# A mixer kernel whose list scheduler also picks the buffers, with the sign step split between GpSimd and VectorE and token weights placed first

## The chip, the core and the metric

The kernel runs on one core of one Trainium2 chip. The metric is the device time of one execution in microseconds (us). The core has five engines with a queue each, taken in order: TensorE (PE, with its weight loads as PEld), VectorE (DVE), ScalarE (ACT), GpSimd (POOL) and SyncE (SP), which here issues nearly all transfers. An instruction waits at the head of its queue until what it needs is there, and all that stand behind it on that engine wait too.

## What is computed

```python
def sm_attn(qq, kk, vv):                      # softmax(qq kk^T / 8) vv
    ...
q_d = q.reshape(B, H, Sd, factor, D).mean(axis=3)        # likewise k_d, v_d
out_up = np.repeat(sm_attn(q_d, k_d, v_d), factor, axis=2)
mask = np.abs(pos[:, None] - pos[None, :]) < factor
...
attn = np.exp(scores)
attn = attn / (np.sum(attn, axis=-1, keepdims=True) + 1e-09)
x = (out_up + np.matmul(attn, v))             # (B, S, H*D)
h = np.maximum(xt @ w_tok1, 0.0) @ w_tok2     # token mixing, xt = x^T
u = x + h.transpose(0, 2, 1)
h2 = np.maximum(u @ w_ch1, 0.0) @ w_ch2       # channel mixing
return (u + h2).astype(np.float32)
```

There are B = 8 batches of H = 8 heads, S = 576 tokens, D = 64, factor = 4 (so Sd = 144 pooled tokens). The token matrices are 576 x 256 and 256 x 576, the channel matrices c1 512 x 1536 and c2 1536 x 512. [...]

## The kernel before, in words

**Precision.** A product in the mixer is done in three passes (`mm3`, L103 to L105): each operand is held as a high and a low part, and high x high, high x low and low x high are summed. Channel mixing takes 16-bit parts (`f16`), token mixing `f32r` parts.

**A batch.** `qk` holds queries and keys, `vw` the values in windows, `vr` the values to be pooled. `pool_q` pools on DVE (L366, L368), `load_v` on POOL (L344, L345). Pooled attention runs over 4 pairs of heads (`pooled`: scores `sd`, maximum `mxd` L386, exponent `pd`, transposes `td` L398, copy `ptd` L401, product `ad` L407, division L413 to L415), and its result goes by a transfer issued on ACT's queue (L421) into `vw`, as one more row of the window. Local attention runs over 5 tiles of tokens (`local`: scores `sc` L439, mask and softmax on DVE L446 to L458, transposes `pT` L462, product `av` L475, copy to `x` L480). Then `mix`: split x into `xh` (L512, L514), product with w_tok1 into `t`, relu and split into `hid` (L529, L531), then for two chunks of 256 and 320 tokens the product with w_tok2 on top of a transpose of x (L545), the copy `u` (L552) and the maximum of |u| (`umx`, L554). `everywhere` brings that maximum to all partitions by two small PE steps (`um_t` L491, `um_b` L497) and two on DVE (L488, L494); `pow2` (L107 to L111) makes a power of two `us` of it, and `uh` is u in two f16 parts (L567 on ACT, L569 on DVE). Channel mixing is `first` (12 blocks f of 12 matmuls into `c`, then `h` on ACT L644 and DVE L646) and `second` (4 blocks c of 36 matmuls from `h` into `c`, then the addition to u, L672, and the store).

**Weights.** A raw tile of 128 x 512 doubles is 512 KB. `to_f32` (L169) takes the high words on ACT (L175), the low words on POOL (L178), and joins them on DVE by a shift (L180); `signed` (L182) adds the sign on DVE (L184). So each tile takes two passes of DVE. Token weights (`token_weight`, 5 pieces of w_tok1 and 4 of w_tok2) are then split into `W` (L213, L215). Channel weights (`Channel.stage`, 12 tiles of C1 and 12 of C2) land in `CW`; PE sums their magnitudes with a matrix of ones (L279, L288), DVE takes the maximum of the sums (L283, L291), and one scale `C_s` for all of C1 (L262 to L264), and one for C2, is used to make the two f16 parts of each tile (`CW`, ACT L268 and DVE L270). W and C1 share the five raw buffers `h`, two loads in flight for each; C2's raw tiles lie in the `vw` buffers.

**What sets the order.** Each part is a generator that yields a `step(engine, us, needs, take, give)` ahead of the instructions it emits. `drive` (L136) keeps model clocks for the engines and picks, again and again, the step that can start first by them, within `PATIENCE` = 0.3 us by the order of the list `streams`. So it writes one fixed order for every engine, from the start until channel products of batch 0 are done (`("over", 0, 1)`): batch 0, all weights, and as much of batch 1 as fits. Its clocks decide the order alone; on the chip every engine takes its queue in that order. PSUM tiles come from three tags, `gg` (2), `m` (3) and `g` (1), which rotate. After `drive`, a plain loop over batches 1 to 7 writes `first` and `second` and puts pieces of the next batch's attention and mixing between the products (`tick`, with `SIDE` = 42).

## Time and profile before

| | us |
|---|---|
| three runs: median (lowest, highest) | 976.34 (975.58, 978.17) |
| the profiled execution's own time | 977.24 |
| its span in the trace | 975.5 |
| time beside the span (977.24 - 975.5) | 1.74 |
| PE busy in the span | 907.9 |
| DVE, ACT, POOL busy in the span | 506.0, 301.1, 112.4 |

The profiled execution took 0.90 us more than the median. In the rows of the profile a group is named by its line, engine, operation, the tile written and the tiles read; "xN" is the number of instructions; a releaser behind "<-" is what ended the idle time before it. A row of windows gives, for a stretch of time, each engine's busy time, then the TensorE clock that was granted, the share of the DMA engines in use and GB/s. The page's second part cuts the span into 40 slices of 24.4 us; a digit is tenths of that slice.

### The profile page before, as it was taken

Reading aid. Unit: us, or ns where it says so; the run is one execution under the profiler, and the core shown is the slowest. Engines: PE = TensorE matmul, PEld = TensorE weight load, DVE = VectorE, ACT = ScalarE, POOL = GpSimd, SP = SyncE. Lnnn points to the kernel's source line nnn. Section 1 sums busy time; section 2 is a strip of 40 time slices with the busy share of each in tenths; the row PEclk is TensorE's granted clock in tenths of the full one; section 3 lists DMA queues with packets and bytes.
Section 4 is the critical chain, followed back from the end, with each engine's and each line's share of the span. In section 5 each row is a group of like instructions: output and inputs, shape, how many; then the busy total and the mean of one; then the engine's idle time right before and its main releaser. Section 6 shows DMA issues by size and latency. Waiting matters only on the chain. (4 is left out here: it accounts for less than half of the span.)

```text
span 975.5 us, 25542 instructions
## 1 busy us (share of the span) xinstructions
PE 907.9 (93%) x11292; PEld 712.2 (73%) x11292; DVE 506.0 (52%) x1187; ACT 301.1 (31%) x627; POOL 112.4 (12%) x213
## 2 busy tenths in 40 slices
PE   5747789999999999999999999999999999999998
PEld 4634467778867778677877778777876778777876
DVE  7879899244645354724555354724645345533221
ACT  1544456212323232422333232422432222322110
POOL 7143500030030003000120003000120000000000
PEclk9976799999999999999999999999999999999999
DMA  8266610530025002500133002600034000000000
GB/s 225 96 234 239 217 31 2 159 90 21 26 61 158 22 8 76 168 7 21 38 107 100 15 14 72 171 1 28 20 84 140 15 15 20 18 2 21 18 12 28
DMA packets 28221, 68.28 MB, mean 70 GB/s; under 512 B 3504, under 2 KB 14000, under 8 KB 26864
## 3 DMA queue, kind: packets, MB, share of 16 engines
q1 hardware_dynamic: 25552, 64.30, 21.9%
q10 hardware_dynamic: 2560, 2.36, 0.9%
q8 instruction: 88, 1.44, 0.6%
q14 instruction: 21, 0.17, 0.1%
HBM read 54.85 MB, written 9.44 MB: 66 GB/s over the span
## 5 line engine op out<-in xcount | busy, mean ns | idle before, releaser
L105 PEld LDWEIGHTS <-CW 128*128 128x128 f16 x4608 | 435.7, 98 | 136.5 <-issue 15.3
L105 PE MATMUL c<-uh,CW 128*128 128x256 f16 (+1 forms) x2304 | 310.7, 288 | 7.0 <-DVE CW L270 4.4
L105 PE MATMUL c<-h,CW 128*128 128x256 f16 (+1 forms) x2304 | 304.5, 287 | 0.8 <-issue 0.7
L646 DVE SCALAR_TENSOR_TENSOR h<-c,h 128x256 f16<-128x256 f32 (+1 forms) x192 | 87.3, 455 | 133.0 <-ACT h L644 131.9
L644 ACT ACTIVATE h<-c 128x256 f16<-128x256 f32 (+1 forms) x192 | 78.4, 408 | 211.2 <-PE c L105 211.0
L344 POOL TENSOR_TENSOR vr<-vr 72x256 f32<-72x256 f32 x64 | 49.0, 765 | 489.4 <-DMA vr<-in_vr_dram 298.1
L672 DVE SCALAR_TENSOR_TENSOR u<-c,io,u 128x256 f32<-128x256 f32 (+1 forms) x64 | 33.0, 516 | 109.7 <-PE c L105 109.7
L554 DVE TENSOR_REDUCE umx<-t 128x1 f32<-128x256 f32 (+1 forms) x64 | 29.2, 457 | 84.5 <-ACT u L552 84.4
L105 PE MATMUL t<-W,hid 128*128 128x256 f32 (+1 forms) x384 | 71.6, 323 | 0.0
L105 PE MATMUL t<-xh,W 128*128 128x512 f32 (+1 forms) x240 | 68.2, 419 | 1.1 <-ACT x L480 0.8
L552 ACT COPY u<-t 128x256 f32<-128x256 f32 (+1 forms) x64 | 25.5, 398 | 119.9 <-PE t L105 119.6
L105 PEld LDWEIGHTS t<-W,hid 128*128 128x128 f32 x384 | 56.7, 200 | 2.6 <-DVE hid L531 0.3
L105 PEld LDWEIGHTS t<-xh,W 128*128 128x128 f32 (+1 forms) x240 | 43.6, 192 | 12.5 <-issue 2.5
L475 PE MATMUL av<-vw,pt 47*32 47x64 f32 x2304 | 37.1, 233 | 14.6 <-ACT pt L466 4.4
L480 ACT COPY x<-av 128x512 f32<-128x512 f32 (+1 forms) x40 | 23.3, 582 | 88.4 <-PE av L475 80.9
L475 PEld LDWEIGHTS av<-vw,pt 47*32 47x32 f32 x2304 | 28.9, 110 | 25.2 <-issue 11.4
L567 ACT ACTIVATE uh<-u,us 128x256 f16<-128x256 f32 (+1 forms) x64 | 29.6, 524 | 49.0 <-DVE us L111 45.0
L407 PE MATMUL ad<-vd,ptd 72*72 72x65 f32 x512 | 42.5, 240 | 0.1
L407 PEld LDWEIGHTS ad<-vd,ptd 72*72 72x72 f32 x512 | 40.5, 157 | 1.3 <-ACT ptd L401 0.4
L545 PEld LDWEIGHTS t<-ident,x 128*128 128x128 f32 (+1 forms) x160 | 22.4, 146 | 18.4 <-issue 9.1
L545 PE MATMUL t<-ident,x 128*128 128x128 f32 (+1 forms) x160 | 33.0, 287 | 2.3 <-DVE umx L554 2.3
L569 DVE SCALAR_TENSOR_TENSOR uh<-u,us,uh 128x256 f16<-128x256 f32 (+1 forms) x64 | 31.1, 537 | 7.6 <-ACT uh L567 7.6
(84 smaller groups left out, 802.6 us busy)
## 6 DMA issues: line engine op xcount, KB each, us to landing
qk<-in_qk_dram SPq DMA_DIRECT2D x32, 579.0 KB
vw<-in_vw_dram SPq DMA_DIRECT2D x32, 351.0 KB
vr<-in_vr_dram SPq DMA_DIRECT2D x64, 144.0 KB
C_raw<-in_c_dram SPq DMA_DIRECT2D x12, 512.0 KB
C_raws<-in_c_dram SPq DMA_DIRECT2D x12, 512.0 KB
out_dram<-u SPq DMA_DIRECT2D x32, 160.0 KB
out_dram<-u SPq DMA_DIRECT2D x32, 128.0 KB
vw<-od ACTq DMA_DIRECT2D x32, 72.0 KB
```

The lines of the kernel that those rows point to most:

```text
L105: nc.tensor.matmul(ps, lhs(a), rhs(c), start=first and i == 0, stop=last and i == 2, **kw)
L344: nc.gpsimd.tensor_add(t[:, 0:2], t[:, 0:2], t[:, 2:4])
L407: nc.tensor.matmul(ps[:, g, par], pt[:, par, kg, G * g:G * g + G], st.vd[:, kg, 2 * pr + par], start=kg == 0, stop=kg == 1)
L475: nc.tensor.matmul(ps[QB * j:QB * j + QB, par, D * hp:D * hp + D], pt[p, hp, QB * j:QB * j + QB], st.vw[h][p, g, D * hp:D * hp + D], start ...
L545: nc.tensor.matmul(ps[:, o:o + n], xf(t)[:, 128 * c:128 * c + 128], ident[:n, :n], start=i == 0, stop=False, is_transpose=True, skip_group ...
L552: nc.scalar.copy(u, ps)
L554: nc.vector.tensor_reduce(umx[:, c:c + 1], ps, axis=AX.X, op=ALU.max, apply_absolute_value=True)
L567: nc.scalar.activation(t[:, 0], us[c], AF.Copy, scale=s)
L569: nc.vector.scalar_tensor_tensor(t[:, 1], us[c], s, t[:, 0], ALU.mult, ALU.subtract)
L644: nc.scalar.activation(ht[:, 0], ps, AF.Relu)
L646: nc.vector.scalar_tensor_tensor(ht[:, 1], ps, 0.0, ht[:, 0], ALU.max, ALU.subtract)
L672: nc.vector.scalar_tensor_tensor(us[c], banks[c], io, us[c], ALU.mult, ALU.add)
```

## The change

The part that `drive` orders is rebuilt; the loop over batches 1 to 7 keeps its form.

- **Buffers.** `drive` picks a numbered buffer for each PSUM tile and for `w` by its own clocks (`slot`, `free`, `held`). The raw tiles of C1 get a pool of their own, `cw` = 6; the token weights keep the five of `h`; of C2's raw tiles four lie in `qk` buffers and eight in `vw`. Loads are streams of their own (`weight_loads`, `Second.loads`), which wait only for a free buffer.
- **Signs.** `to_f32` does the sign by one instruction more, on POOL for every second tile (L214, which writes the sign bits of the 64-bit word's top 16 bits) and on DVE for the others (L217); then one DVE instruction (L219) joins and writes the result where it belongs.
- **Scales.** The sums of channel tiles are sums of squares (L304, L323). C1 has a scale for each quarter of four tiles (`First.scale`), and its f16 parts (L291, L293) are made a quarter at a time; C2 has one scale, after C1's. C2's f16 parts have a place of their own (`CX`, `CY`, in the `cw` buffers and one more).
- **Setup.** `masks` take 10 selects and 2 copies on POOL in place of 26 selects, and `rep` is a DVE sum (L105) in place of 8 selects.
- **Junk products.** `keep_busy` (L146 to L151) puts products of a tile of ones into PSUM tile `busy` that nobody reads, 14 at the start and up to 8 before a PE step for which the model clock shows a gap, until the last `uh` of batch 0.
- **Mixing.** `mix` is four generators (`splits`, `products`, `takes`, `scaled`). In `products` all of a batch's products with w_tok2 come in a row, and the maximum's way through PE (`um_t` L554, `um_b` L560) is in another.
- **Order.** The streams stand as loads, token weights, the tail of channel mixing, mixing, then C1, attention and the rest; `PATIENCE` is 0.15; the model's costs differ; `drive` ends when also batch 1's first `uh` is made.

```diff
-PATIENCE = 0.3
+SG = 2
+PATIENCE = 0.15
...
+    def keep_busy(n):
+
+        if n:
+            ps = P1("busy")
+            for _ in range(n):
+                nc.tensor.matmul(ps, junk[:, :128], junk, start=True, stop=True)
...
-            if e == "P" and ("uh", 0, 0) not in made:
-                us *= 1.8
+            if e == "P" and ("uh", 0, 1) not in made and free["g"]:
+                keep_busy(min(8, int((t - clock["P"]) * 0.6 / 0.22)))
...
-    def to_f32(raw, at):
+    def by_pool():
+        count[0] += 1
+        return count[0] * SG % 4 < SG
+
+    def to_f32(raw, at, y=None, *needs):
...
         nc.gpsimd.tensor_scalar(lo, lo, 2.0 ** -29, -0.501, ALU.mult, ALU.add)
-        yield step("V", 0.08 + n * 0.0012)
-        nc.vector.scalar_tensor_tensor(lo, hi, 3, lo, ALU.logical_shift_left, ALU.bitwise_or)
...
-        nc.vector.scalar_tensor_tensor(y, words[:, :, 1], 0x80000000, words[:, :, 0],
-                                       ALU.bitwise_and, ALU.bitwise_or)
+        if by_pool():
+            yield step("G", 0.08 + n * 0.0026)
+            nc.gpsimd.tensor_scalar(top, hi.bitcast(F32), 2.0 ** -126, 2.0 ** -126, ALU.mult, ALU.mult)
+        else:
+            yield step("V", 0.08 + n * 0.0015)
+            nc.vector.scalar_tensor_tensor(lo, hi, 0x80000000, lo, ALU.bitwise_and, ALU.bitwise_or)
+        e = yield step("V", 0.08 + n * 0.0012, *needs)
+        nc.vector.scalar_tensor_tensor(lo if y is None else y(), hi, 3, lo, ALU.logical_shift_left, ALU.bitwise_or)
...
+        def scale(self):
+            for q in range(NQ):
+                yield from self.norms(q)
+                big = yield from everywhere(f"C1_n{q}", self.mx[:, q:q + 1])
+                e = yield step("V", 0.45, give="g")
+
+                self.root(big, 2.0 ** (4.5 + 0.5 - 8), self.inv[q], self.s[q])
+                make(("C1", "scale", q), e)
+                for i in range(4 * q, 4 * q + 4):
+                    yield from self.parts(i)
...
-        streams = [pool_all(st), load_v(st), windows(st)] + attend(0) + [mix(st), up]
-        streams += [w1s, C1.stage(), w2s, C2.stage(("av", 0, last))]
...
+        streams = [x for k in "LWUMTSaCDPHmQAh" for x in group[k]]
+        left = drive(streams, [("over", 0, 1)] + [("uh", 1, 0)] * (B > 1))
```

Three places show how the instructions move. The first is DVE, where the last tiles of C1 are joined, the scale of C1 comes out and the first f16 parts are made. Before, with `h_0_0` three rows further on:

```order
L283 TENSOR_REDUCE C_mx<-C_sum_1139 128x1
L569 SCALAR_TENSOR_TENSOR uh_1_0_1267<-u_1_0_1170,us_1_1258,uh_1_0_1267 128x320
L262 TENSOR_REDUCE C_big<-C_mx 128x1
L109 TENSOR_SCALAR C_inv<-C_big 128x1
L110 TENSOR_SCALAR C_inv<-C_inv 128x1
L111 RECIPROCAL C_s<-C_inv 128x1
L569 SCALAR_TENSOR_TENSOR uh_1_1_1274<-u_1_1_1196,us_1_1258,uh_1_1_1274 128x320
L184 SCALAR_TENSOR_TENSOR CW_198<-C_raws 128x512
L569 SCALAR_TENSOR_TENSOR uh_1_2_1281<-u_1_2_1213,us_1_1258,uh_1_2_1281 128x320
L270 SCALAR_TENSOR_TENSOR CW_176<-CW_177,C_s,CW_176 128x512
L569 SCALAR_TENSOR_TENSOR uh_1_3_1286<-u_1_3_1235,us_1_1258,uh_1_3_1286 128x320
L180 SCALAR_TENSOR_TENSOR C_raws<-C_raws 128x512
```

Now, on the same engine, with the second product of batch 0's mixing still to come (`xh_4` is the last piece of x):

```order
L282 TENSOR_SCALAR C_inv_121<-C_n_b 128x1
L284 TENSOR_SCALAR C_inv_121<-C_inv_121 128x1
L285 RECIPROCAL C_s_124<-C_inv_121 128x1
L217 SCALAR_TENSOR_TENSOR W_raw<-W_raw 128x288
L219 SCALAR_TENSOR_TENSOR CW_142<-C_raw 128x512
L219 SCALAR_TENSOR_TENSOR W_raw<-W_raw 128x288
L293 SCALAR_TENSOR_TENSOR CW_134<-CW_135,C_s_124,CW_134 128x512
L239 TENSOR_TENSOR W_1_154<-W_raw,W_1_154 128x288
L219 SCALAR_TENSOR_TENSOR CW_143<-C_raw 128x512
L293 SCALAR_TENSOR_TENSOR CW_135<-CW_136,C_s_124,CW_135 128x512
L217 SCALAR_TENSOR_TENSOR C_raw<-C_raw 128x512
L580 TENSOR_TENSOR xh_4_1076<-x_4_1062,xh_4_1076 64x512
```

The f16 parts of C1 (L270, now L293) begin with the first quarter's scale, while tiles CW_142 and CW_143 of C1 are still being joined (L219) and the token weights W are being split; before they began when all 12 tiles of C1 had been joined and after `uh` of the second chunk had begun.

The second place is POOL at the end of C1's tiles and the start of C2's (`C_raws`). Before, there was one instruction for a tile:

```order
L178 TENSOR_SCALAR W_raw<-W_raw 128x288
L178 TENSOR_SCALAR C_raws<-C_raws 128x512
L178 TENSOR_SCALAR C_raw<-C_raw 128x512 x2
L178 TENSOR_SCALAR C_raws<-C_raws 128x512
L178 TENSOR_SCALAR C_raw<-C_raw 128x512
L178 TENSOR_SCALAR C_raws<-C_raws 128x512 x2
```

Now every second tile has L214 behind its L211:

```order
L214 TENSOR_SCALAR C_raw<-C_raw 128x512
L211 TENSOR_SCALAR C_raw<-C_raw 128x512 x2
L214 TENSOR_SCALAR C_raw<-C_raw 128x512
L211 TENSOR_SCALAR C_raw<-C_raw 128x512
L211 TENSOR_SCALAR C_raw_1014<-C_raw_1014 128x512
L214 TENSOR_SCALAR C_raw_1014<-C_raw_1014 128x512
L211 TENSOR_SCALAR C_raw_1016<-C_raw_1016 128x512
L211 TENSOR_SCALAR C_raw_1018<-C_raw_1018 128x512
L214 TENSOR_SCALAR C_raw_1018<-C_raw_1018 128x512
L211 TENSOR_SCALAR C_raw_1021<-C_raw_1021 128x512
L211 TENSOR_SCALAR C_raws_1053<-C_raws_1053 128x512
```

All told, 16 instructions of L214 stand in POOL's queue, 12 of them of 128x512.

The third place is DVE where one batch passes into the next (batch 4 behind batch 3). Before:

```order
L488 TENSOR_REDUCE um_0_m<-umx_0_6986 128x1
L672 SCALAR_TENSOR_TENSOR u_1_0_5701<-c_3_1_0_7051,io_1_7050,u_1_0_5701 128x320
L494 TENSOR_REDUCE um_0_m_7108<-um_0_t 1x1
L109 TENSOR_SCALAR ui_0_7112<-um_0_b 128x1
L110 TENSOR_SCALAR ui_0_7112<-ui_0_7112 128x1
L111 RECIPROCAL us_0_7113<-ui_0_7112 128x1
L569 SCALAR_TENSOR_TENSOR uh_0_0_7117<-u_0_0_6996,us_0_7113,uh_0_0_7117 128x256
L569 SCALAR_TENSOR_TENSOR uh_0_1_7120<-u_0_1_7022,us_0_7113,uh_0_1_7120 128x256
L569 SCALAR_TENSOR_TENSOR uh_0_2_7136<-u_0_2_7049,us_0_7113,uh_0_2_7136 128x256
L569 SCALAR_TENSOR_TENSOR uh_0_3_7139<-u_0_3_7074,us_0_7113,uh_0_3_7139 128x256
```

Now:

```order
L629 TENSOR_REDUCE umx_1_7354<-t_4_1_0_7245 128x1 x2
L629 TENSOR_REDUCE umx_1_7354<-t_4_1_2_7306 128x1 x2
L751 SCALAR_TENSOR_TENSOR u_1_2_5918<-c_3_1_2_7292,io_1_7160,u_1_2_5918 128x320
L557 TENSOR_REDUCE um_0_m_7362<-um_0_t 1x1
L551 TENSOR_REDUCE um_1_m<-umx_1_7354 128x1
L118 TENSOR_SCALAR ui_0_7382<-um_0_b 128x1
L119 TENSOR_SCALAR ui_0_7382<-ui_0_7382 128x1
L120 RECIPROCAL us_0_7383<-ui_0_7382 128x1
L648 SCALAR_TENSOR_TENSOR uh_0_0_7390<-u_0_0_7174,us_0_7383,uh_0_0_7390 128x256
L648 SCALAR_TENSOR_TENSOR uh_0_1_7396<-u_0_1_7221,us_0_7383,uh_0_1_7396 128x256
L648 SCALAR_TENSOR_TENSOR uh_0_2_7411<-u_0_2_7281,us_0_7383,uh_0_2_7411 128x256
```

Before, the chain from `um_0_t` to `uh_0` stood ahead of three of the four sums `u_1` of the old batch (u_1_0 to u_1_3); now it stands behind three of them, and both chunks' maxima (`umx_1` too) come before it. On PE, 38 (batch 2) to 128 (batch 7) matmuls stood between `um_0_b` and the first product with the batch's `uh_0` before; now 8 stand there in batch 2, and 21 to 31 in batches 3 to 7.

More of the change, by code (lines that the diff above doesn't have):

```diff
@@ L111, in pow2 @@
         nc.vector.reciprocal(s, inv)
-    clock = dict.fromkeys("AGVPSD", 0.0)
+    clock = dict(A=2.0, G=5.0, V=2.0, P=0.0, S=0.0, D=0.0)
     now = [0.0]
-    free = dict(gg=[0.0] * 2, m=[0.0] * 3, g=[0.0], w=[0.0] * 4)
+    free = {k: {i: 0.0 for i in range(n)} for k, n in SLOTS.items()}
+    held = {}
     made = {}
@@ L134, in fetched @@
         return clock["D"] + 2.0
+    def keep_busy(n):
[3 more added lines that the diff above has]
+                nc.tensor.matmul(ps, junk[:, :128], junk, start=True, stop=True)
     def drive(streams, until):
         items = [[g, next(g, None), 0.0] for g in streams]
-        while until not in made:
+        driven[0] = True
+        while not all(u in made for u in until):
             some = []
@@ L166, in drive @@
                 it[1] = None
+        driven[0] = False
+        for k, n in SLOTS.items():
+            first = min(free[k], key=free[k].get) if free[k] else [i for (x, _), v in held.items() for i in v if x.split(">")[0] == k][0]
+            now_in[k] = (first - 1) % n
         return [it for it in items if it[1] is not None]
-    def to_f32(raw, at):
+    count = [0]
+    def by_pool():
+        count[0] += 1
+        return count[0] * SG % 4 < SG
+    def to_f32(raw, at, y=None, *needs):
         n = raw.shape[1] // 2
@@ new lines, in token_weight @@
+    def token_weight(i, n, f):
+        yield step("A", 0.0, ("W", "raw", i))
+        raw = made["W", "raw"][i]
+        yield from to_f32(raw, made["W", "raw", i])
+        y = raw.rearrange("p (n two) -> p n two", two=2)[:, :, 0].bitcast(F32)
+        yield step("A", 0.1 + n * 0.0011)
+        nc.scalar.copy(f[:, 0], y)
+        e = yield step("V", 0.08 + n * 0.0012)
+        nc.vector.tensor_tensor(f[:, 1], y, f[:, 0].bitcast(F32), ALU.subtract)
+        make(("W", "y", i), e)
+        make(("W", "read", i), e)
@@ L600, in ahead @@
     def ahead(b):
-        yield step("S", 0.1, *([("mixed", 0)] if b == 1 else []))
+        yield step("S", 0.1, *([("C2", "read", i) for i in range(4)] + [("pair", 0, 3)] if b == 1 else []))
         st = load(b)
@@ L618, in side @@
             if b + 1 < B:
-                yield from together([m, ahead(b + 1)], 2)
-            else:
-                yield from m
+                m.append(ahead(b + 1))
+            yield from together(m, len(m))
     def first(st, ch, places):
@@ L679, in through, with second_weights @@
             yield from g
-    def scale_out():
-        yield step("V", 0.1, ("C2", NF - 1))
-        nc.vector.tensor_mul(ic, C1.inv, C2.inv)
     def main(st, places):
         banks = [], []
-        up = through(first_up(st, 0), first_up(st, 1), scale_out(), second_up(st, 0, banks[0]),
-                     second_up(st, 1, banks[1]))
-        return [up, through(first(st, 0, places[0]), first(st, 1, places[1]),
-                            second(st, 0, banks[0]), second(st, 1, banks[1]))]
+        up = [first_up(st, 0), first_up(st, 1), through(second_up(st, 0, banks[0]), second_up(st, 1, banks[1]))]
+        return up, [first(st, 0, places[0]), first(st, 1, places[1]),
+                    through(second(st, 0, banks[0]), second(st, 1, banks[1]))]
+    def second_weights():
+        yield step("S", 0.0, *(("C1", "read", i) for i in range(NF)))
+        C2.place = pairs("CX") + singles(1, "CY")
+        make(("C2", "places"), now[0])
+        yield from C2.scale()
     def lazily(what, *needs):
```

441 lines of the change are left out of this document (238 added, 203 removed).

## The prediction, made before the changed kernel was run

> **What bounds it now.** I read the page's busy times first, then its slices (tenths of 24.4 us each), a table of windows, DVE's waits, and last the timelines of DVE and PE at the places where the slices change.
>
> ```profile
> PE 907.9 (93%) x11292; PEld 712.2 (73%) x11292; DVE 506.0 (52%) x1187; ACT 301.1 (31%) x627; POOL 112.4 (12%) x213
> ...
> PE   5747789999999999999999999999999999999998
> ...
> DVE  7879899244645354724555354724645345533221
> ```
>
> PE is busy for 907.9 of 975.5 us, and in every slice from the seventh on it is at 9 tenths. The slack lies in the first six slices, where DVE's digits are the higher ones.
>
> ```profile
> 60.00:120.00 60.00, 38.44 (x173) 25.23 (x171) 52.25 (x90) 24.93 (x49) 27.15 (x35) 0.69 0.67 239
> 120.00:140.00 20.00, 15.50 (x190) 11.26 (x191) 19.41 (x41) 9.94 (x18) 4.28 (x5) 1.00 0.22 45
> 140.00:160.00 20.00, 19.98 (x365) 16.12 (x364) 18.85 (x46) 12.96 (x26) 0.00 (x0) 1.00 0.01 2
> 412.00:524.00 112.00, 109.39 (x1402) 86.14 (x1402) 54.83 (x135) 33.27 (x70) 9.58 (x17) 1.00 0.21 60
> ```
>
> From 140 on PE has no gap, and in a steady stretch of 112 us (one batch) it is busy for 109.39, so 2.6 us a batch are idle. From 60 to 120 it is busy for 38.4 of 60 us, at a granted clock of 0.69, and DVE for 52.3. So two questions set the time: when DVE lets PE run without gaps, and how much PE has to do from then on.
>
> ```profile
> 92.29 0.86 DVE L569 SCALAR_TENSOR_TENSOR uh<-u,us,uh 128x256 f16<-128x256 f32 x1
> ...
> 109.22 0.16 DVE L111 RECIPROCAL C_s<-C_inv 128x1 f32<-128x1 f32 x1
> ...
> 168.09 0.74 DVE L270 SCALAR_TENSOR_TENSOR CW<-CW,C_s,CW 128x512 f16<-128x512 f32 x1
> ```
>
> ```profile
> 110.20 0.61 PE L105 MATMUL c<-uh,CW 128*128 128x256 f16 x2 [2.31 <-ACT CW L268]
> 112.30 2.74 PE L105 MATMUL c<-uh,CW 128*128 128x256 f16 x12 [1.49 <-DVE CW L270]
> ...
> 168.37 1.20 PE L407 MATMUL ad<-vd,ptd 72*72 72x65 f32 x16
> ...
> 171.04 2.78 PE L105 MATMUL c<-h,CW 128*128 128x256 f16 x24
> 174.86 0.27 PE L475 MATMUL av<-vw,pt 47*32 47x64 f32 x2 [1.04 <-DMA vw<-od]
> 175.64 1.78 PE L475 MATMUL av<-vw,pt 47*32 47x64 f32 x126 [0.51 <-DMA vw<-od]
> ```
>
> The last `uh` of chunk 0 is ready at 93.2 (92.29 + 0.86), but the first channel product starts at 110.20: C1 has one scale (`C_s`, 109.22), which waits for all its 12 tiles, and the next product waits for DVE's `CW` again. The last f16 part of C2 is ready at 168.8; PE starts the second product (c<-h) at 171.04 with its queue full, and waits twice in it for a transfer (1.04 and 0.51).
>
> ```profile
> 0.00:115.10 115.10, 72.35 (x900) 53.69 (x900) 93.10 (x192) 46.02 (x91) 46.19 (x101) 0.82 0.63 206
> 115.10:168.80 53.70, 48.78 (x679) 36.98 (x680) 50.97 (x111) 31.59 (x59) 8.94 (x11) 0.97 0.14 32
> ```
>
> Up to that last part DVE is busy for 93.10 + 50.97 = 144.1 us and idle for 24.7, of which 22.0 lie before 115.1. These are the two numbers that the change works on.
>
> **The sum.** The point I work out is R, when DVE has made the last f16 part of C2. Behind R the products of c2 need nothing more from the start-up.
>
> *DVE's work up to R.* The rows, with their count and mean in ns:
>
> ```profile
> L184 DVE SCALAR_TENSOR_TENSOR CW<-C_raw 128x512 uint32<-128x512 uint32 x12 | 9.4, 781 | 0.2
> ...
> L283 DVE TENSOR_REDUCE C_mx<-C_sum 128x1 f32<-128x512 f32 x3 | 2.0, 682 | 0.0
> ...
> L184 DVE SCALAR_TENSOR_TENSOR W_raw<-W_raw 128x256 uint32<-128x256 uint32 x4 | 2.0, 508 | 0.1
> ...
> L494 DVE TENSOR_REDUCE um_m<-um_t 1x1 f32<-1x128 f32 x2 | 0.5, 270 | 0.0
> ...
> L110 DVE TENSOR_SCALAR C_inv<-C_inv 128x1 f32<-128x1 f32 x2 | 0.3, 154 | 0.1
> ```
>
> Twelve of the 24 signs of channel tiles go to POOL: 12 x 0.78 = 9.4 us. Four of nine token pieces go too, at 0.508: 2.0. Added are two more maxima of sums (six instead of four, 2 x 0.68 = 1.4); four ways of a scale across the partitions, each 0.27 and four small steps of 0.15, so 0.9, where two stood with four small steps each (3.6 - 1.2 = 2.4); six small steps that carry C1's scales into C2's (0.9); the sum that makes `rep` (0.5, under the 0.68 of L283, which reads four times as much). Net 11.4 - 5.2 = 6.2 us less. Joining (L180, now L219) and the f16 parts (L270, now L293) stay as many as they were. I cost at nothing the fewer set-up instructions on POOL, which lie before any weight is there, and the sums of squares on PE (96 small matmuls in place of 60 of the old sums), which PE's gaps of 21.6 us from 60 to 120 hide; uncovered, 36 more would be some 5 us at the 0.14 of a steady product's matmul.
>
> *What POOL's work costs DVE.*
>
> ```profile
> L178 POOL TENSOR_SCALAR C_raws<-C_raws 128x512 uint32<-128x512 uint32 x12 | 9.9, 827 | 16.9 <-DMA C_raws<-in_c_dram 11.8 <-ACT u L552 4.5
> ```
>
> ```profile
> 93.23 1.02 POOL L178 TENSOR_SCALAR C_raw<-C_raw 128x512 uint32<-128x512 uint32 x1 [0.35 <-DMA C_raw<-in_c_dram]
> ```
>
> ```profile
> 93.07 0.68 DVE L184 SCALAR_TENSOR_TENSOR CW<-C_raw 128x512 uint32<-128x512 uint32 x1
> ...
> 93.67 1.11 DVE L180 SCALAR_TENSOR_TENSOR C_raws<-C_raws 128x512 uint32<-128x512 uint32 x1
> ```
>
> L214 isn't in this trace; its nearest row is L178 with 0.83, the same engine and size and also two operations. Sixteen of them (four on half tiles, halved) are 14 x 0.83 = 11.6 us of POOL. DVE pays beside it: its join takes 1.11 while L178 runs (93.23 to 94.25), and a pass of the same size that is nearly clear of it 0.68, so up to 0.43 for one. Ends: 0 when L214 falls where DVE waits, 14 x 0.43 = 6 when each meets one DVE instruction. I take 3, since DVE is busy for 4 of 5 us there and not every pass is hit. As for POOL itself: 24 tiles and 12 more at 0.83 make 30 us, in a stage of some 80 (from about 40, where raw tiles begin, to 120, where the last is joined), so L214 would have to take over 4 us before C2 waits for POOL.
>
> *DVE's idle time up to R.* Its list, us and times:
>
> ```profile
> DVE W_raw L180 <- POOL W_raw L178: 4.1, 3, 3.0
> DVE umx L554 <- ACT u L552: 3.9, 2, 2.8
> DVE hid L531 <- ACT hid L529: 2.0, 1, 2.0
> DVE h L646 <- ACT h L644: 1.6, 4, 0.8
> DVE P L101 <- POOL rep L72: 1.5, 1, 1.5
> DVE C_raw L180 <- POOL C_raw L178: 0.9, 1, 0.9
> ```
>
> ```profile
> SPq L189 <- DVE W L215: 21.4, 4, 9.4
> ```
>
> ```profile
> 97.19 1.97 PE L105 MATMUL t<-W,hid 128*128 128x320 f32 x6
> ...
> 103.34 1.14 PE L105 MATMUL t<-W,hid 128*128 128x320 f32 x6
> ```
>
> `rep` comes from DVE itself (1.5 gone). The waits for raw tiles come from loads that SP holds back until a buffer is free (21.4 us of SP's time until DVE is done with W); with six buffers for C1 alone and loads ahead of all, I take away 3 of 4.1, and C_raw's 0.9. `umx` and `hid` wait for products on a slow PE: the same six matmuls take 1.97 at 97 and 1.14 at 103. Junk products stand in such gaps now; I take away 2 of 3.9 and 1 of 2.0. `h` waits (1.6) lose half. That is 9.2, so 15.5 us of idle are left. Ends: nothing goes (the new order brings as many waits as it removes), and 8 are left. The junk itself costs nothing where PE has a gap anyway; at worst, where the model's gap isn't there, eight of them (0.53 each, 1.97 / 6 for 320 columns taken to 512) hold up a product by 4 us.
>
> By the Trainium skill ("TensorE: Matmul & The Clock Gate", Part 1) the clock is released only after about 3.4 us of sustained work and falls back after an idle window as long; the granted 0.69 would fit a mix of its two states. By that rule eight junk products are barely enough, the 3 us of `umx` and `hid` would stay, and the sum would come out at 964, inside the forecast's own range below.
>
> R = 144.1 - 6.2 + 3 + 15.5 = 156.4, against 168.8.
>
> *Does PE get there first?* Its work from the first product to the start of c2 is 48.8 (115.1 to 168.8), 3.4 before and 2.2 behind it. The first product now needs C1's first quarter only, and so starts with the last `uh`, at about 93 again (more f16 parts ahead of it, less idle). That gives 93 + 54 = 147, plus 3.5 for c2 matmuls that now stand ahead of the last tile: 151 at most. DVE, at 156.4, is later and decides.
>
> *Behind R.* Before, PE needs 975.5 - 171.04 = 804.5 us from the start of c2. Now 30 of the 36 matmuls of its first block stand ahead of the last tile (30 x 2.78 / 24 = 3.5 off), the last pooled product `ad` stands behind (about 1.2 as 16 small matmuls, on), and the two waits for its transfer (1.55) become about 0.5 longer, for less stands between. 802.7.
>
> *Between batches.*
>
> ```profile
> 548.12 0.38 PE L497 MATMUL um_b<-um_m,ones 1*128 1x1 f32 x2
> 548.43 0.99 PE L105 MATMUL c<-h,CW 128*128 128x320 f16 x6
> ```
>
> ```profile
> 548.54 0.16 DVE L109 TENSOR_SCALAR ui<-um_b 128x1 uint32<-128x1 uint32 x1 [0.49 <-PE um_b L497]
> ...
> 549.72 1.68 DVE L569 SCALAR_TENSOR_TENSOR uh<-u,us,uh 128x256 f16<-128x256 f32 x4 [0.64 <-ACT uh L567]
> ```
>
> From `um_b` to the first `uh` pass 2.0 us (549.72 and a quarter of 1.68), to the last 3.3. The new order has 21 or more matmuls behind `um_0_b` in batches 3 to 7, at 0.99 / 6 each 3.4 us of cover: nothing is paid. Batch 2 has 8, 1.2 us of cover: 0.9 paid.
>
> Span: 156.4 + 802.7 + 0.9 = 960.0. With the 1.74 beside it 961.7, and less the 0.90 by which the profiled execution stood above the median, **961**. With the contention at its ends and 11 to 19 us of idle left, this case runs from 955 to 967.
>
> **The rivals.** *PE decides:* if the waits shrink to 8 and L214 meets nothing, DVE is ready at 145.9, and PE at about 148 to 151; 149 + 802.7 + 0.9 + 0.8 = 953. For it speaks that C1's 17 us of waiting (93.2 to 110.2) have a single cause, which is gone; against it that the 24.7 us of idle time have a dozen small causes, and no one edit answers more than three of them.
>
> *POOL shuts DVE out:* each L214 stops DVE for its whole length: 11.6 instead of 3, R = 165.0, and 969. The rows speak against the whole of it (1.11 beside POOL's 1.02 is 0.43 more, not 1.02 more). The Trainium skill ("SBUF — State Buffer", SBUF: two separate sides) states this mechanism: one exclusive lock for GpSimd and a VectorE instruction with two SBUF inputs, held for the whole instruction. All of L180, L184 and L270 have two.
>
> *New waits for old:* idle stays at 24.7, R = 165.6, 970. Together with the rival before: 174.2, and 979, which is no change.
>
> *Slower, by the batch boundary:* the maxima of both chunks now pass DVE behind three sums `u_1`, which wait for c2 blocks. If PE must sit through the whole chain, 3.3 us at six boundaries are 19.8 instead of 0.9, and 980. It decides from 2.7 us a boundary on ((976.3 - 961 + 0.9) / 6). Against it: 3.4 us of cover at five of the six.
>
> **Chances.** 0.3% (2.9 us) is about what a measurement of this kernel can tell from no change. The forecast has 0.48, PE deciding 0.15, POOL shutting DVE out 0.12, new waits alone 0.05: faster 0.80. The two together, no change: 0.09. The boundary and what else costs more than 20 us: 0.11. The range from 950 to 972 takes in the first four.
>
> **What would show it.** Right: `rep` and most raw-tile waits gone from DVE's list; the first product (c<-uh) at 90 to 97; the last f16 part of C2 at 152 to 161, PE without gaps from then on; about 109.4 busy in 112 us later. L214 at 0.6 to 0.9. Wrong: PE idle by over 1 us at each `c_b_0_0`; f16 parts at 1.2 us or more beside L214 (the lock); a last part past 165; channel products that wait for DVE while POOL works on.

## The result and the profile after

| | before | after |
|---|---|---|
| median of the runs on one chip (lowest, highest), us | 976.95 (975.58, 978.17) | 960.93 (960.28, 961.48) |
| profiled execution, us | 977.24 | 961.2 |
| its span, us | 975.5 | 959.0 |
| first channel product of batch 0, us | 110.2 | 101.0 |
| from there to the end of the span, us | 865.3 | 858.0 |
| last f16 part of C2 ready (R), us | 168.8 | 159.8 |

The ratio is 0.9836 (0.9819 to 0.9853). Of the 16.5 us that the span lost, 9.2 lie ahead of the first channel product and 7.3 behind it. The page of the changed kernel:

```profile
PE 916.6 (96%) x11427; PEld 708.1 (74%) x11427; DVE 499.9 (52%) x1191; ACT 301.6 (31%) x627; POOL 132.3 (14%) x204
...
PE   8588898999999999999999999999999999999998
DVE  7699998326472364525554273724555264523221
```

From the third to the sixth slice DVE is at 9 tenths (7, 9, 8 and 9 before) and PE at 8, 8, 8 and 9 tenths (4, 7, 7 and 8 before). The table of windows for two of the stretches shown of before:

```profile
60.00:120.00 60.00, 49.70 (x352) 34.73 (x352) 57.04 (x110) 32.54 (x65) 36.15 (x36) 0.86 0.51 171
...
412.00:524.00 112.00, 110.37 (x1417) 86.68 (x1415) 54.31 (x135) 33.26 (x72) 9.41 (x17) 1.00 0.20 59
```

From 60 to 120 PE does 49.7 us of work instead of 38.4, at a granted clock of 0.86 instead of 0.69. The steady 112 us hold 110.37 of work where 109.39 were, so the loop over batches has changed too. Next the two parts of the start-up, cut at the first channel product and at the last f16 part of C2; behind them DVE's timeline at both points, and PE's:

```profile
0.00:101.00 101.00, 76.16 (x997) 48.14 (x998) 85.44 (x179) 46.14 (x89) 58.38 (x79) 0.86 0.67 205
101.00:159.83 58.83, 56.02 (x759) 44.45 (x757) 55.46 (x127) 31.44 (x62) 17.18 (x23) 0.97 0.31 81
```

```profile
100.49 0.47 DVE L648 SCALAR_TENSOR_TENSOR uh<-u,us,uh 128x256 f16<-128x256 f32 x1
...
159.08 0.74 DVE L293 SCALAR_TENSOR_TENSOR CX<-CY,C_s,CX 128x512 f16<-128x512 f32 x1
```

```profile
101.02 2.76 PE L114 MATMUL c<-uh,CW 128*128 128x256 f16 x12
```

DVE's busy time up to R (159.08 + 0.74) is 85.44 + 55.46 = 140.90 us, the forecast's figure. Its idle time is 159.83 - 140.90 = 18.9 us, not 15.5. The first product starts when the last `uh` of chunk 0 is ready (100.49 + 0.47). At the start of c2, PE's timeline has no wait:

```profile
155.48 2.79 PE L114 MATMUL c<-h,CX 128*128 128x256 f16 x24
158.80 1.48 PE L114 MATMUL c<-h,CX 128*128 128x256 f16 x12
```

The last twelve of the first block's 36 matmuls, which read the last tiles of C2, run from 158.80 to 160.28, and R is 159.82. So R holds up nothing that shows, though only by a narrow margin, and PE, at work for 56.0 of the 58.8 us ahead of R, sets the time from the first product on. Windows of PE's work from there to the end, before and after:

```profile
110.20:975.50 865.30, 838.90 (x10406) 660.28 (x10406) 417.59 (x1002) 257.62 (x541) 70.91 (x118) 0.99 0.18 52
```

```profile
101.02:959.00 857.98, 840.46 (x10432) 659.95 (x10430) 414.42 (x1013) 255.44 (x538) 73.88 (x125) 1.00 0.19 55
```

The work is the same (838.9 and 840.5 us); the idle time fell from 26.4 to 17.5. DVE's list of waits up to 160 shows what made `uh` late:

```profile
DVE W L239 <- ACT W L237: 7.5, 1, 7.5
DVE h L725 <- ACT h L723: 1.7, 2, 1.2
...
DVE W_raw L217 <- POOL W_raw L211: 0.7, 2, 0.3
...
DVE umx L629 <- PE C_sum L323: 0.4, 1, 0.4
```

`umx` (3.9 before, 0.4 now), `W_raw` (4.1, 0.7), `hid`, `rep` and `C_raw` (2.0, 1.5 and 0.9, not in the list now) have lost 11.3 us together, more than the 9.2 that the forecast took off for these and `h`. A wait of 7.5 us that was not there has come. ACT's and then DVE's timeline at that place:

```profile
31.16 9.58 ACTq L484 DMA_DIRECT2D vw<-od  x4
```

```profile
41.79 0.43 DVE L239 TENSOR_TENSOR W<-W_raw,W 128x256 fp32r<-128x256 f32 x1 [7.46 <-ACT W L237]
```

ACT needs 9.58 us to issue four transfers (`vw<-od`, L484), and the copies behind them in its queue wait. From 0 to 40 the DMA engines are 92% in use in the mean (70% before). DVE stands at L239, which wants ACT's `W`, and behind it wait the softmax passes of batch 0, whose x the mixing, and so `uh`, needs.

In the loop three of PE's waits from 250 to 960 were, before:

```profile
PE av L475 <- ACT x L480: 2.0, 5, 0.4
...
PE av L475 <- issue: 1.5, 3, 1.0
...
PE c L105 <- issue: 0.7, 1, 0.7
```

and after, all that is left:

```profile
PE td L461 <- ACT pd L454: 3.6, 5, 0.8
PE pT L525 <- DVE P L521: 2.6, 5, 1.2
PE av L538 <- DMA vw<-od: 1.3, 3, 0.6
```

The whole list of before comes to 13.1 us; these three rows to 7.5. Its waits for `x` and the "issue" waits, in which PE waited for nothing that the profile shows, are gone.

### The profile page after: what moved, and what is told of

Same layout as the page of the kernel before. It is cut to its first block, busy times and chain, and to the rows that moved or that the text cites. A ratio compares the mean times of both kernels' runs of the same rounds, so it can differ in the third digit from the quotient of the medians.

```text
span 959.0 us, 25814 instructions
## 1 busy us (share of the span) xinstructions
PE 916.6 (96%) x11427; PEld 708.1 (74%) x11427; DVE 499.9 (52%) x1191; ACT 301.6 (31%) x627; POOL 132.3 (14%) x204
## 3 DMA queue, kind: packets, MB, share of 16 engines
q8 instruction: 89, 1.46, 0.6%
## 5 line engine op out<-in xcount | busy, mean ns | idle before, releaser
L114 PE MATMUL c<-h,CX 128*128 128x256 f16 (+1 forms) x2304 | 307.8, 287 | 0.0
L114 PEld LDWEIGHTS <-CW 128*128 128x128 f16 x2304 | 217.0, 98 | 69.8 <-issue 16.2
L114 PEld LDWEIGHTS <-CX 128*128 128x128 f16 x2304 | 216.9, 98 | 58.7 <-issue 1.5
L114 PE MATMUL t<-W,hid 128*128 128x256 f32 (+1 forms) x384 | 67.5, 310 | 0.1
L114 PEld LDWEIGHTS t<-W,hid 128*128 128x128 f32 x384 | 53.2, 188 | 2.5 <-DVE C_n_m L551 0.3
L538 PE MATMUL av<-vw,pt 47*32 47x64 f32 x2304 | 36.0, 232 | 9.5 <-DVE P L509 5.6
L538 PEld LDWEIGHTS av<-vw,pt 47*32 47x32 f32 x2304 | 28.3, 109 | 20.5 <-issue 10.3
L470 PE MATMUL ad<-vd,ptd 72*72 72x65 f32 x512 | 38.9, 228 | 1.9 <-issue 1.2
L470 PEld LDWEIGHTS ad<-vd,ptd 72*72 72x72 f32 x512 | 36.7, 145 | 4.1 <-issue 2.8
L509 DVE TENSOR_TENSOR P<-sc,mask 128x304 f32<-128x304 f32 (+1 forms) x40 | 18.7, 468 | 27.7 <-PE sc L502 26.7
```

The lines of the kernel that those rows point to most:

```text
L114: nc.tensor.matmul(ps, lhs(a), rhs(c), start=first and i == 0, stop=last and i == 2, **kw)
L470: nc.tensor.matmul(ps[:, g, par], pt[:, par, kg, G * g:G * g + G], st.vd[:, kg, 2 * pr + par], start=kg == 0, stop=kg == 1)
L538: nc.tensor.matmul(ps[QB * j:QB * j + QB, par, D * hp:D * hp + D], pt[p, hp, QB * j:QB * j + QB], st.vw[h][p, g, D * hp:D * hp + D], start ...
```

## The experiments

Each ratio is to the kernel before on the same chip; the changed kernel's is 0.9836. A hundredth is 9.8 us. Diffs are against the changed kernel unless said otherwise.

**Why is the loop shorter?** The forecast spoke of one edit there, the maximum's way through PE. Two others reach batches 2 to 7: the model's costs of the steps of scores (0.45 and 0.7 became 0.6 and 1.0, which spaces them among channel products) and the four streams of mixing. Each was put back alone, then both.

```diff
-yield step("P", 0.6, ("q", b, pr), ...
+yield step("P", 0.6 if b < 2 else 0.45, ("q", b, pr), ...
-yield step("P", 1.0, ("q", b, 3), ...
+yield step("P", 1.0 if b < 2 else 0.7, ("q", b, 3), ...
```

> The changed kernel with one thing put back: from batch 2 on, the cost that a step of pooled scores has for the filling of the loop is 0.45 again (not 0.6), and that of local scores 0.7 (not 1.0). The start-up's order is the same to the last instruction. Two theories on the 6.7 us that PE was idle less between 240 and 955. Theory 'loop': they are a gain of the loop's new order, and the costs, which set how many channel products are put between two attention steps, are one half of its cause; then PE's named waits after 250 us go from 7.5 towards 13 us and the time from 961 to 963 to 967. Theory 'moved': the loop is no better, batch 1's mixing was just done earlier; then 960 to 962.

```diff
-            m = mix(st)
+            m = [mix_in_row(st)]
```

> The changed kernel with mixing in the loop (batches 2 to 7) in one row again as before, instead of four generators side by side. The start-up's order is the same. Theory 'loop' (four generators let the second chunk's products and the split of x go ahead while a wait is on): 963 to 967, and PE's waits on x and on the second attention product come back. Theory 'moved': 960 to 962.

> Both at once: the changed start-up with the loop as before (costs and mixing). Theory 'loop': 966 to 968, so the start-up by itself is worth 9 to 11 of the 16 us. Theory 'moved': 960 to 962, and the start-up is worth all 16.

The old costs alone took 978.35 us (970.41 to 982.15), 0.9990 (0.9957 to 1.0022): the whole gain is gone. The old row of mixing took 962.29, 0.9848 (0.9823 to 0.9873), no effect that these runs can tell. Both took 974.94, 0.9969 (0.9940 to 0.9998). The first and the third took longer than the 963 to 968 that were expected. So it is the costs. With the old costs the first product comes at 103.5, and 868.7 us pass from there to the end, against 858.0; so the loss lies mostly in the loop, where PE's list of waits has a new head:

```profile
PE av L538 <- issue: 5.5, 3, 2.5
PE c L114 <- issue: 3.6, 3, 1.4
```

That is 9.1 us of issue waits, where the changed kernel has none.

The same two numbers were then put into the kernel before, with nothing else of the change:

```diff
-        yield step("P", 0.45, ("q", b, pr), ...
+        yield step("P", 0.45 if b < 2 else 0.6, ("q", b, pr), ...
-        yield step("P", 0.7, ("q", b, 3), ...
+        yield step("P", 0.7 if b < 2 else 1.0, ("q", b, 3), ...
```

> The kernel before with one thing of the change: the two costs of attention steps in the loop (0.6 and 1.0 in place of 0.45 and 0.7), from batch 2 on; start-up unchanged. If these two numbers are what the loop gained, PE's named waits after 250 us fall from 13 to under 9 and the time to 0.993 to 0.997 of the kernel before. Rival: they only help the new loop, which had other waits: 0.998 to 1.002.

It took 972.31 (970.31 to 975.13), 0.9948 (0.9927 to 0.9968), about 5 us faster, as expected; PE's waits from 250 to 960 come to 8.2 us there. Of the 715 us from 240 to 955 PE worked for 705.2:

```profile
240.00:955.00 715.00, 705.21 (x8830) 553.19 (x8829) 331.90 (x819) 205.33 (x442) 46.73 (x85) 1.00 0.17 50
```

In the same window it worked for 700.2 in the kernel before and for 706.9 in the changed one.

So the costs are worth some 5 us in the old order and some 13 to 15 in the new (the intervals leave room for 10 to 20), which without them meets stops that the old one met less.

**What are the issue waits?** The theory: PE's list of instructions comes late when loads fill the DMA engines. First the next batch's loads were put behind its mixing in the program, with the old costs.

```diff
-                m.append(ahead(b + 1))
-            yield from together(m, len(m))
+                yield from together(m, len(m))
+                yield from ahead(b + 1)
```

> The first experiment's kernel (old costs in the loop), with one thing more: the loads of the next batch begin when mixing is through, not beside it. If PE's waits for nothing shown (9.1 us after 240 in that profile) are late packets of instructions that stand behind these loads, they fall under 2 and the time from 978 to 962 to 968. Rival: attention's small matmuls stand so densely that PE outruns any fetch: the waits stay over 6 us and the time at 974 to 980.

It took 972.91 (971.11 to 973.9), 0.9938 (0.9918 to 0.9959). The issue waits were still there:

```profile
PE c L114 <- issue: 6.8, 4, 2.2
PE av L538 <- issue: 3.7, 2, 3.0
```

SP starts a load as soon as its buffer is free, and so this did not move them away from the small products. One such stop in PE's timeline:

```profile
496.29 0.86 PE L538 MATMUL av<-vw,pt 47*32 47x64 f32 x64
...
500.23 0.94 PE L114 MATMUL c<-h,CX 128*128 128x256 f16 x7 [2.21 <-issue]
```

and the one packet of the instruction queue q8 from 497 to 498, while loads hold the DMA engines at 99%:

```profile
q8 instruction: 1, 0.02, 6.0%
```

It starts at 497.9, and PE goes on 2.3 us later. At the stop that ends at 722.96 the packet starts at 720.6 (2.4 us). Then the loads were really held, by a copy of a value of the batch before into the tile that is to be loaded (the load overwrites it).

```diff
+            if b > 2:
+                nc.scalar.copy(t[:1, :1], ready[b - 1].ui[1][:1])
```

> As the experiment before it (old costs in the loop, next loads behind mixing), but now the loads of queries and keys really wait: from batch 3 on one value of the last batch's scale (made at the end of its mixing) is copied into each tile ahead of its load, which overwrites it. In the experiment before, SP started them as soon as attention's last scores had freed the tiles, whatever stood before them in the program, so it did not test the fetch. If PE's waits for nothing shown are packets of instructions that stand behind these loads, they fall from 10.5 us to under 3 and the time to 0.985 to 0.990 of the kernel before. Rival: attention's small matmuls outrun any fetch; the waits stay over 6 us and the time at 0.994 or more.

It took 974.45 (972.41 to 979.38), 0.9968 (0.9946 to 0.9989). The issue waits fell to 1.8, as that theory said, but the time did not, since the late loads make waits of their own (here and below L540 is the L538 of the changed kernel):

```profile
PE av L540 <- DMA vw<-od: 4.5, 5, 1.3
PE sd L445 <- DVE qd L433: 4.1, 7, 0.9
PE av L540 <- issue: 1.8, 3, 0.8
```

The same place as above, in this kernel, has the same products as close together, and no stop:

```profile
505.81 0.86 PE L540 MATMUL av<-vw,pt 47*32 47x64 f32 x64
506.60 1.97 PE L114 MATMUL c<-h,CX 128*128 128x256 f16 x16
```

From 504 to 508 the DMA engines are 52% in use there, against 88% from 495 to 499 in the kernel that stops. The changed kernel, with the new costs, has them at 82% beside the same product (495 to 499) and doesn't stop either: there the product before it lies 3.5 us ahead and not 1.55. So these stops need both, dense small products and loads beside them, and either edit removes most of them; that spacing the products also gains time is shown by the costs, not by this run.

**What are the signs, the junk and the quarters worth?** A caution ahead of these. Six of the profiled kernels have one and the same order on every engine for the first 227 us: the changed one, the three with a loop put back, and the two with late loads. Yet their first product comes at 100.0, 101.0, 103.4, 103.5, 103.9 and 104.9, and R lies between 158.7 and 162.8; an early stop of PE (1.2 to 6.9 us long, see the last two kernels) differs among them. So a difference of up to 5 us in the start-up of two profiles can't be put down to an edit. First all signs on DVE:

```diff
-SG = 2
+SG = 0
```

> The changed kernel with all signs on DVE (SG = 0), none on POOL; the list scheduler makes a new order of it. By the forecast's terms DVE gets 11.4 us of signs back and loses 3 us of slowing by POOL, so the last f16 part of C2 comes 8 us later than at 159.8 and the time is 966 to 970. Rival (the measured 1.5 us of L214, beside which DVE's passes take 0.86 to 1.1 us instead of 0.68, cost DVE as much as the signs did): 959 to 963.

It took 973.22 (968.87 to 975.88), 0.9952 (0.9929 to 0.9974), about 11 us of the gain. The first product comes at 113.6 and 857.6 us pass from there to the end, as in the changed kernel: the loss lies in `uh`, which is 12.5 later. R is 180.0, with DVE busy for 146.5 and idle for 33.5, so the extra work is 5.6 and the rest idle time, which the list of DVE's waits names:

```profile
DVE rd L476 <- PE ad L470: 7.3, 1, 7.3
DVE CX L293 <- ACT CX L291: 7.2, 3, 5.4
```

The first is PE standing still in a pooled product (7.45 us, see the last two kernels), which is not the signs' doing; the 7.5 us wait for `W` is 2.8 here. The kernel with the old row of mixing has both of these nearly alike (6.4 and 2.8), and its profiled execution took 964.75, against 972.87 here: some 8 us are left for the signs and the order that comes with them. The time is longer than either forecast.

Then no junk product anywhere (`keep_busy` does nothing):

```diff
-        if n:
+        if n < 0:
```

> The changed kernel without any junk product; the order of all else is the same. By the forecast's terms 3 us of waiting on slow products come back: about 964. Rival: PE's instructions are fetched in packets of 16 KB beside the loads, and the 87 junk products use 174 of them; PE's waits for nothing shown (issue) before 60 us, 2.9 in the changed kernel and 6.4 to 8.0 in the first experiments' profiles, then shrink to under 2, the slow products cost less than that, and the time is 956 to 960.

It took 965.34 (964.3 to 967.1), 0.9867 (0.9841 to 0.9893): about 3 us, though the two intervals overlap. The first product is 1.2 later (102.2), which is inside the scatter, and 860.3 us pass from there. The rival's condition came true (one issue wait of 1.4 us before 60) and its gain did not. What junk does to the granted clock can be read here, with the order the same (0.86 with junk):

```profile
60.00:120.00 60.00, 45.35 (x309) 34.12 (x308) 55.21 (x106) 31.28 (x63) 31.79 (x34) 0.73 0.49 169
```

Then one scale for all of C1:

```diff
-                big = yield from everywhere(f"C1_n{q}", self.mx[:, q:q + 1])
...
+            big = yield from everywhere("C1_n", self.mx)
+            e = yield step("V", 0.45, give="g")
+            self.root(big, 2.0 ** (4.5 + 0.5 - 8), self.inv[0], self.s[0])
```

> The changed kernel with one scale for all of C1, taken when all 12 tiles are joined, in place of one for each quarter; the list scheduler makes a new order. If the first channel product comes earlier because of the quarters, it goes from 101 back to 108 or later, the last f16 part of C2 (159.8) comes 3 to 8 us later, and the time is 964 to 969. Rival: DVE's work sets the end of C2 anyway and the order in which it is done doesn't matter: last part within 1.5 us of 160, 960 to 963.

It took 965.32 (964.88 to 969.15), 0.9874 (0.9844 to 0.9903), inside the expected range, but by luck: the first channel product, which was to carry the loss, did not move, and the interval overlaps that of the changed kernel. PE's timeline:

```profile
86.56 0.38 PE L561 MATMUL C_n_b<-C_n_m,ones 1*128 1x1 f32 x2 [0.80 <-DVE C_n_m L558]
...
100.91 1.25 PE L114 MATMUL c<-uh,CW 128*128 128x256 f16 x10
```

The one scale passes PE at 86.6, 14 us ahead of the first product, which waits for `uh` as in the changed kernel. In the kernel before the one scale came at 109.2. So C1's tiles are joined some 20 us earlier, and with that the product can start without the quarters. What loss there is lies behind it (861.9 us to the end, R at 166.0); no single wait there accounts for it.

**Can the 7.5 us wait go?** Three loads of C1 in flight at most, in place of six, were to free the DMA engines:

```diff
+        most = 3 if tag == "cw" else BUFS[tag]
-            yield step("S", 0.1, *([(name, "read", i - BUFS[tag])] if i >= BUFS[tag] else []))
+            yield step("S", 0.1, *([(name, "read", i - most)] if i >= most else []))
```

> The changed kernel with at most three raw tiles of C1 in flight, not six; new order from the list scheduler. ACT's four transfers of pooled rows take 9.6 us to issue at 31 us (4.8 in three of the first experiments) while the DMA engines are 97% in use, and DVE, POOL and PE wait for ACT behind them. If full DMA queues are the cause, the issue falls to 3.5 or less, DVE's wait for ACT's W from 7.5 to under 2.5, and the time to 955 to 959. Rival: fewer loads ahead bring the waits for raw tiles back (W_raw, C_raw over 3 us in DVE's list), 961 to 966.

The ratio is 0.9902 (0.9866 to 0.9938), from executions of 968.27 to 970.64; a fourth took 1730.66, for which the record has no cause, and isn't in the ratio. This is slower than both forecasts. ACT's issue took 3.5 us and the wait for `W` 1.8, but the scheduler made another order of it: the first product came at 91.4, R at 174.2, with waits of DVE for `h` (5.7) and `CX` (4.7). From the first product 877.5 us pass to the end: up to 175 PE waits for a transfer (6.3), for instructions (4.0) and for `uh` (2.7). With fewer loads in flight the issue and the wait are shorter; what that alone is worth this run can't say.

Next the transfers of batch 0 went to SP's queue, so that ACT does not hold them:

```diff
-                    nc.scalar.dma_start(st.vw[h][...
+                    (nc.sync if b == 0 else nc.scalar).dma_start(st.vw[h][...
```

> The changed kernel with batch 0's four transfers of pooled rows issued from SP and not from ACT; the order of all else is the same. In the changed kernel ACT is held by them for 9.6 us (4.8 to 5.8 in other profiles) and DVE waits 7.5 for ACT's W. If this is the part of the idle time that the forecast missed, DVE's wait falls under 1, the last f16 part of C2 comes 2 to 4 us before 159.8, and the time is 0.979 to 0.982 of the kernel before (the changed kernel has 0.984). Rival: on SP they stand behind loads that wait for buffers, the second attention product comes later by 3 us or more, and nothing is gained: 0.983 or more.

It took 963.65 (961.61 to 964.22), 0.9849 (0.9826 to 0.9872): nothing gained, as the rival had it. DVE's wait for `W` is gone, but its idle time in the first 40 us is 13.8 against 11.7, because PE stops for 6.28 us in a pooled product:

```profile
25.57 0.87 PE L470 MATMUL ad<-vd,ptd 72*72 72x65 f32 x6 [6.28 <-issue]
```

The first packet of q8 starts between 22.4 and 22.6 there:

```profile
q8 instruction: 1, 0.02, 46.0%
```

In the changed kernel PE stops after the same tenth matmul of that product, for 1.16 us, and the first q8 packet starts between 16.6 and 16.8:

```profile
19.59 0.54 PE L470 MATMUL ad<-vd,ptd 72*72 72x65 f32 x6 [1.16 <-issue]
```

```profile
q8 instruction: 1, 0.02, 43.1%
```

In both, PE goes on 2.9 to 3.05 us after the packet's start, as in the eight more of these kernels that stop there. The long stop isn't the transfers' doing, then: in four kernels with the start-up of the changed one, transfers on ACT, it is 5.6 to 6.9 us. Up to it PE's windows count 222 matmuls and 223 weight loads in both kernels. PE stops at a fixed place until its list arrives, and how long depends on when the packet starts. Fewer instructions ahead of that point should help, and the 36 junk products ahead of it are such. So the last kernel keeps the transfers on SP and puts junk only behind batch 0's pooled attention:

```diff
-            if e == "P" and ("uh", 0, 1) not in made and free["g"]:
+            if e == "P" and ("pair", 0, 3) in made and ("uh", 0, 1) not in made and free["g"]:
...
-        keep_busy(14)
```

> The experiment before it (batch 0's transfers of pooled rows issued from SP) with junk products only after pooled attention of batch 0, none in the opening. In the profiles of the changed order DVE is idle for 11 to 14 us in the first 40, in two waits that take turns: for a pooled product that stands still in PE's instruction list (1.2 to 7.4), and for ACT behind its transfers (2.8 to 7.5). If both are real and separate, this kernel has neither: DVE's idle time before 40 falls to 6 to 9, the last f16 part of C2 comes at 154 to 157, and the time is 0.978 to 0.982 of the kernel before. Rival: the first 40 us are set by the loads (DMA engines 97% in use from 20 to 40), and a wait that goes is waited elsewhere; then DVE's idle time stays at 11 to 14 and the time at 0.983 to 0.988.

**955.72 us** (954.35 to 956.51), 0.9758 (0.9737 to 0.9779), faster than both kernels, and than the forecast. The first 40 us in the changed kernel, and in this one:

```profile
0.00:40.00 40.00, 30.15 (x482) 17.76 (x482) 28.29 (x74) 11.23 (x20) 19.71 (x44) 0.95 0.92 262
```

```profile
0.00:40.00 40.00, 27.89 (x439) 21.80 (x440) 31.49 (x80) 13.55 (x25) 20.16 (x48) 1.00 0.91 254
```

DVE is idle for 8.5 of them instead of 11.7, and PE has no stop in the pooled product, though the first packet starts at 21.6. The column of the clock, 1.00 here, is not to be read as a faster PE. One of the pooled products, in the changed kernel and in this one:

```profile
15.68 1.25 PE L470 MATMUL ad<-vd,ptd 72*72 72x65 f32 x16
```

```profile
15.16 2.18 PE L470 MATMUL ad<-vd,ptd 72*72 72x65 f32 x16
```

Without the opening junk PE is slower, so two things keep it from the stop: less stands ahead of it, and PE works off what does more slowly (212 matmuls up to 24.4). The run doesn't separate them, and the late junk was not tried with the transfers on ACT. The first channel product comes 3.6 us earlier:

```profile
97.38 2.57 PE L114 MATMUL c<-uh,CW 128*128 128x256 f16 x12
```

The span is 954.7, so 857.3 us pass from there to the end, and R is 155.8.

## Why the prediction was right, and where it was not

The time, 961, was right, but not by its own sum: two misses cancel. R came 3.4 us later than forecast (159.8 for 156.4), what lies behind R was 4.4 shorter (799.2 for 803.6), and R itself no longer decided.

*"DVE, at 156.4, is later and decides"* is the step that failed. PE decides, as in the first rival, only later than that rival had it: from the first product to the start of c2 it takes 54.46 us (101.02 to 155.48, forecast 54), but it starts at 101 and not at 93. In seven of the eight kernels with the new order and costs, the span less the time of the first product is 857 to 862 us (858.0 in the changed kernel and with the old row of mixing, 857.6 with all signs on DVE, 860.3 without junk, 861.9 with one scale, 860.5 and 857.3 in the last two), while the first product moves from 97.4 to 113.6. So what the start-up is worth is read from the last `uh` of chunk 0, as long as the rest keeps up with it. The kernel with three loads in flight is the one where it did not (first product at 91.4, R at 174.2, 877.5 us): the early first product gained nothing there.

*The first product* does start with that `uh`, as the forecast has it, and the 17 us of waiting behind it are gone. But `uh` is 7.8 us later than before (101.0 for 93.2), where "at about 93 again" was forecast and 90 to 97 named as a sign of being right: DVE now joins C1's tiles and makes f16 parts ahead of it, and the 7.5 us wait lies ahead of it too. The reason given, the quarters, was wrong: with one scale the product comes at the same time.

*DVE's work*, 140.9, came out as forecast, but by terms that cancel. L214 takes 1.5 to 1.6 us in the mean, not 0.83:

```profile
L211 POOL TENSOR_SCALAR C_raw<-C_raw 128x512 uint32<-128x512 uint32 x16 | 16.4, 1028 | 1.3
L214 POOL TENSOR_SCALAR C_raw<-C_raw 128x512 bf16<-128x512 f32 x8 | 12.9, 1611 | 8.8 <-ACT C_raw L208 8.4
L211 POOL TENSOR_SCALAR C_raws<-C_raws 128x512 uint32<-128x512 uint32 x8 | 6.0, 752 | 10.8 <-DMA C_raws<-in_c_dram 9.5 <-DVE h L725 0.8
L214 POOL TENSOR_SCALAR C_raws<-C_raws 128x512 bf16<-128x512 f32 x4 | 5.8, 1461 | 6.6 <-ACT C_raws L208 6.5
```

What it costs DVE was forecast at 3. The timelines show more. One L214 on POOL, the f16 part that DVE begins beside it, and the next f16 part, beside which POOL does nothing:

```profile
106.50 1.35 POOL L214 TENSOR_SCALAR C_raws<-C_raws 128x512 bf16<-128x512 f32 x1 [2.51 <-ACT C_raws L208]
```

```profile
106.48 1.63 DVE L293 SCALAR_TENSOR_TENSOR CW<-CW,C_s,CW 128x512 f16<-128x512 f32 x1
...
110.89 0.73 DVE L293 SCALAR_TENSOR_TENSOR CW<-CW,C_s,CW 128x512 f16<-128x512 f32 x1
```

An f16 part of 1.2 us or more beside L214 was named as a sign of being wrong, and here is one. Ten passes of DVE over 512 elements a row, with two inputs from SBUF, begin beside an L214, 0.6 us or more ahead of its end, and outlast it. They take 0.91 to 1.63 us, and each ends 0.25 to 0.28 us after that L214. An eleventh runs inside an L214 in its usual 0.68, and there it is L214 that takes 2.45. Over the shortest pass of their form (0.67 to 0.73) they are 6.3 us longer in all. So the mechanism of the rival "POOL shuts DVE out" is there, and the lock of the Trainium skill ("SBUF — State Buffer", SBUF: two separate sides) fits these passes. Its price is not: by the rival each L214 would cost its whole length, 18.7 us for those of 128 x 512. An estimate, with the shortest pass of each form as its undisturbed time: up to R DVE's passes are stretched by 13.4 us before and by 18.1 after, 4.7 more where 3 were forecast, and the undisturbed work fell by 7.9 where 6.2 were. The two misses, 1.7 each, cancel.

*Idle time*, "15.5 us of idle are left", was 18.9. The named waits went, by more than forecast, but ACT, held by its own transfers, made a new one: the rival "new waits for old", in part. With the transfers moved it is gone, and PE's long stop for instructions stands in its place, as it does in other profiles of the changed start-up.

*The signs* were priced by DVE's passes, 11.4 us. With all of them on DVE its work up to R is 5.6 us more, and `uh` is 12.5 later; so more than half of the difference is idle time. PE's longer stop for instructions adds some 6 us of it, the shorter wait for `W` takes nearly 5 back, and how the rest splits between the signs and the order that the scheduler then makes stays open.

*Junk products* were priced at 3 us (2 for `umx`, 1 for `hid`). Without them `umx` waits for 1.8 us instead of 0.4, and `hid` isn't in the list either way, so most of the 3 us went with the new order and not by junk. Some 3 us of time are lost without junk (the intervals overlap), and no wait accounts for them. The reading by the Trainium skill's clock gate ("TensorE: Matmul & The Clock Gate", Part 1), by which those 3 us would stay, did not come true; the granted clock from 60 to 120 is 0.86 with junk and 0.73 without.

*"Between batches"* failed by omission. It priced the way of the maximum and found next to nothing, rightly: none of the three waits left in PE's list is for `uh` or `um_b`, and the slower rival falls. But it passed over two changed numbers in the planner, which take several us from the loop.

The parts don't add up: taken out singly the costs are worth 15 us, the signs 11 (some 8 beside PE's longer stop), the quarters 4 and the junk 3, twice the 16 of the whole, and the last two are no larger than the runs can tell. What stays open is how the gain ahead of the first product splits among buffers, masks and order, which were not tried singly, and why some kernels scatter by 10 us (970 to 982 with the old costs) and others by less than 2.

## What to carry to other kernels

Read a planner's costs as part of a change: two numbers that nobody waits for gave 5 us in the old kernel, and without them the new one's whole gain was gone. When loads are brought forward, look at what else uses the DMA engines: here the engine that issued transfers beside the loads stood still for longer, and so did an engine whose instructions had to come by them. And when a wait is removed, ask what comes next at that spot before counting the gain: moving the transfers alone brought nothing, with the opening junk gone as well it brought 5 to 8 us more than the change.

## What the runs showed of the hardware

**An engine can run out of instructions.** q8 moves 16 KB a packet (89 packets, 1.46 MB); PE has 11427 matmuls and as many weight loads, so a packet is about 256 instructions of 64 bytes. In ten profiled kernels PE stood still at the start for 1.16 to 7.45 us, each time until 2.9 to 3.05 us after the first packet began. In the loops with the old costs it stood still, in 13 of 14 stops of 1 us or more, until 2.2 to 2.5 us after one. At the stop shown above 64 small products with their weight loads had passed in 0.86 us, and loads filled the DMA engines. The Trainium skill ("Runtime: NRT & Kernel Launch", Instruction fetch mechanics) has the blocks of 16 KiB and 256 instructions, and the trace agrees; it calls the cost of crossing one mostly hidden, and here up to 10.5 us in the loop were not.

**Issuing a transfer can take 2.4 us.** Four transfers of 72 KB took ACT 3.44 us where the DMA engines were 33% in use meanwhile (the kernel before), 3.46 at 50% (three loads in flight), 4.78 at 58% (old costs), 4.94 at 70% (late loads), 5.80 at 80% (no junk) and 9.58 at 91% (the changed kernel).

**A pass of POOL can hold up DVE.** DVE's passes of 128 x 512 that began beside an L214 took up to 1.63 us instead of 0.73, and ended 0.25 to 0.28 us after it.

**L214 costs 1.6 to 1.9 times its neighbour on POOL.** It reads every second 32-bit float and writes every fourth 16-bit word (1.61 us for `C_raw` and 1.46 for `C_raws`); L211 takes 1.03 and 0.75 for the same tiles.
